# Loads issued three attention tiles ahead of use, with buffers dealt anew and the order rebuilt

## The chip, the cores and the metric

The kernel runs on one core of one Trainium2 chip. A time is the device time of one execution in microseconds (us). Medians are over the executions named; the fast executions of one kernel lie within about 1.5% of each other here. A run counts as slow when it is over 1.5% above the fastest run of the same kernel; slow runs are left out of every comparison. Traces are of one execution each. The span of a trace is some 1.7 us shorter than the time of the same execution (287.6 against 289.32 us in before).

## The reference, cut to what matters

Block-sparse attention over 4 batches of 8 heads, 768 tokens, head size 64; its output, as 3,072 rows of 512, goes through a two-layer network with a swish-like gate.

```python
scores = scale * np.matmul(q, k.transpose(0, 1, 3, 2))
scores = np.where(mask, scores, -1e9)          # mask of 32x32 blocks, from an input
attn = softmax(scores)                          # along the keys
x = np.matmul(attn, v)                          # -> [3072, 512]
h = x @ w_in                                    # [3072, 2048]
out = (h * sigmoid(beta * h)) @ w_out           # [3072, 512]
```

## The kernel before

Two heads make a pair; there are 16 pairs, numbered 0 to 15, four to a batch. A pair's K, Q and V are loaded as float32 (384 KB each), cast to float16 on VectorE (DVE) or GpSimd (POOL), and K and Q are transposed, by TensorE (PE) for the first four pairs and by the DMA engines for the rest. A tile is 256 or 512 queries of one pair; it takes 3 or 6 score steps (scores on PE, exponential on ScalarE (ACT), mask on DVE), then the product with V, a normalization on DVE and a transpose of the result. Batches are numbered from zero. As soon as enough tokens are done, the network's two layers run on PE: "up" with `w_in`, "down" with `w_out`.

The program is a list of nodes. A greedy builder, `order_of`, sorts them with a model of durations, buffers and DMA rates before anything runs. It takes the node with the smallest modelled start plus a bias for its kind. The program then gives each engine its nodes strictly in that order. So changing a bias, a buffer count or a modelled size rebuilds the order on all engines.

```python
BIAS = {"mask": -288, "spread": 115, "beta": 289, "weights": 285, "load": 963, "cast": 110, ...}
W_GATE = (2, "k")
SLOTS = {"st_k": 3, "st_q": 4, "st_v": 3, "s16_k": 2, "s16_q": 3, "set": 6, "va": 7,
         "et": 12, "xst": 4, "recip": 4, "t_sb": 4, "g": 2, "osb": 3, "sc": 2, "mm": 4}
# st_*: float32 stagings of loads; s16_*: float16 casts; set: transposed K and Q of a pair;
# va: V in float16; xst: attention output; osb: final output

def order_of(nodes, free, slots):
    ...
                key = (n_start + n.dur[e] - min(n.dur.values()) + bias, n.place)
                if best is None or key < best[0]:
                    best = (key, n, e, n_start)
    ...

def add_weights(gate):                 # W_GATE: the load after which the weights start
    st, load = gate
    def shut():                        # a tiny op that waits for that load
        nc.gpsimd.tensor_copy(out=w_in_sb[0:1, 0, 0:1], in_=at(st)[0:1, 0, 0:1])
    gate = add("weights", "POOL", 600, 50, shut, deps=[load], use=[st])
    ...                                # then four loads of weights from POOL's queue, 1 MB each
                                       # as written in float16

def add_load(nm, x, st, lo, hi, gate): # from SP's queue
    ...
    deps = [(last_load[0], -1e9)] if last_load else []
    ...
    last_load[:] = [add("load", "SP", ..., load, deps=deps,
                         moved=65536 * (hi - lo) + ..., **kw)]

for x in range(NPAIR):                 # batch zero: K, part of Q, V of pairs 0..3
    add_prep(x)
add_weights(loads[W_GATE])
for x in range(NPAIR):                 # the rest of Q of pairs 0..3
    add_rest(x)
for x in range(NPAIR, len(pairs)):     # all other pairs: as early as buffers allow
    add_prep(x, (0, 1, 1) if x == NPAIR else (None, None, None))
...
for b, q0, n in tiles:
    for j in range(NPAIR):
        ...                            # score steps and tail of one tile
```

The softmax here doesn't subtract the row's maximum and nothing guards it: scores larger than these inputs give would overflow.

## Time and profile before

| | before |
|---|---|
| time, median of 3 | 291.43 us (290.86 to 291.66) |
| span of the trace | 287.6 us |
| PE busy | 265.2 us, idle 22.4 us |
| DVE, ACT busy | 209.4 us, 212.9 us |

The page of the kernel before: first busy time, share of the span and count of instructions; then 40 equal slices of 7.2 us, each digit the busy share in tenths; PEclk is the granted clock of PE in tenths, DMA the busy share of the DMA engines, GB/s what they moved.

```profile
span 287.6 us, 6162 instructions
...
PE 265.2 (92%) x2455; PEld 138.1 (48%) x2455; DVE 209.4 (73%) x429; ACT 212.9 (74%) x277; POOL 27.6 (10%) x46
...
PE   4767899979895999899999999999999999999994
...
PEclk9998999999999999999999999999999999999999
DMA  7999987999999997771227201021002111011112
GB/s 205 291 232 214 212 182 197 279 237 223 230 269 234 252 282 153 173 164 28 76 73 131 55 2 55 20 93 55 1 2 73 39 43 43 0 21 73 39 44 105
```

PE is full from about 120 us on. Up to about 108 us, while the DMA engines move mostly 200 to 290 GB/s, it is not. The busy time in chosen stretches (start:end and length, then busy us of PE, PEld, DVE, ACT and POOL with counts, granted clock, DMA share, GB/s) says how much is missing where:

```profile
20.00:41.00 21.00, 17.91 (x193) 12.00 (x194) 17.47 (x43) 18.81 (x31) 0.87 (x3) 0.92 1.15 212
41.00:60.00 19.00, 17.79 (x209) 9.33 (x205) 17.74 (x39) 16.81 (x21) 2.13 (x4) 1.00 1.00 220
60.00:120.00 60.00, 52.86 (x506) 26.09 (x505) 46.52 (x90) 44.96 (x56) 10.80 (x12) 1.00 1.13 229
120.00:279.00 159.00, 159.00 (x1416) 81.23 (x1414) 113.69 (x216) 119.75 (x159) 4.16 (x5) 1.00 0.21 54
```

From 60 to 120 us PE lacks 7.1 us. The timeline (start, duration, engine, line, operation, in brackets the engine's idle time before it and what ended it) shows the largest piece:

```profile
88.72 0.56 DVE L394 CAST va<-st_v 128x768 f16<-128x768 f32 x1 [4.72 <-DMA st_v<-in_v_dram]
...
89.20 0.42 DVE L522 TENSOR_TENSOR xst<-mm,recip 128x256 f16<-128x256 f32 x1
...
89.67 2.89 PE L586 MATMUL mm<-w_out_sb,g 128*128 128x512 f16 x12 [3.27 <-DVE xst L522]
...
92.92 1.94 ACT L468 ACTIVATE et<-sc 128x1024 f16<-128x1024 f32 x2 [4.76 <-PE sc L460]
```

DVE stood 4.72 us before the cast of a V, because its load had not landed (it did at 88.70 us). The normalization `xst` that stood behind the cast in DVE's order came only at 89.20; it releases a PSUM buffer, and the down matmuls of PE waited 3.27 us for that. This V belongs to pair 10, whose first scores come at about 137 us: nobody needed the cast yet. In this trace the mask and normalization work behind the cast did not pass it: DVE stood idle for those 4.72 us, and `xst` began 0.48 us after the cast.

### The profile page before, as it was taken

Reading aid. Unit: us, or ns where it says so; the run is one execution under the profiler, and the core shown is the slowest. Engines: PE = TensorE matmul, PEld = TensorE weight load, DVE = VectorE, ACT = ScalarE, POOL = GpSimd, SP = SyncE. Lnnn points to the kernel's source line nnn. Section 1 sums busy time; section 2 is a strip of 40 time slices with the busy share of each in tenths; the row PEclk is TensorE's granted clock in tenths of the full one; section 3 lists DMA queues with packets and bytes.
Section 4 is the critical chain, followed back from the end, with each engine's and each line's share of the span. In section 5 each row is a group of like instructions: output and inputs, shape, how many; then the busy total and the mean of one; then the engine's idle time right before and its main releaser. Section 6 shows DMA issues by size and latency. Waiting matters only on the chain.

```text
span 287.6 us, 6162 instructions
## 1 busy us (share of the span) xinstructions
PE 265.2 (92%) x2455; PEld 138.1 (48%) x2455; DVE 209.4 (73%) x429; ACT 212.9 (74%) x277; POOL 27.6 (10%) x46
## 2 busy tenths in 40 slices
PE   4767899979895999899999999999999999999994
PEld 1545575443362365346455336363345454466741
DVE  5878888998966586999688886587877686852600
ACT  1688997999863777897888997679976888824621
POOL 4520101111431001113001000000000000000000
PEclk9998999999999999999999999999999999999999
DMA  7999987999999997771227201021002111011112
GB/s 205 291 232 214 212 182 197 279 237 223 230 269 234 252 282 153 173 164 28 76 73 131 55 2 55 20 93 55 1 2 73 39 43 43 0 21 73 39 44 105
DMA packets 72850, 36.66 MB, mean 127 GB/s; under 512 B 29796, under 2 KB 68724, under 8 KB 72820
## 3 DMA queue, kind: packets, MB, share of 16 engines
q1 hardware_dynamic: 69568, 32.06, 49.0%
q0 software_dynamic: 3136, 4.19, 8.2%
q8 instruction: 19, 0.31, 0.5%
q14 instruction: 11, 0.09, 0.1%
q10 hardware_dynamic: 116, 0.01, 0.0%
HBM read 27.27 MB, written 6.29 MB: 117 GB/s over the span
## 4 chain that ended last, share of the span: by engine, by line
PE 71%; DMA 13%; DVE 7%; SPq 3%; ACT 2%; issue 1%; POOL 0%; DVEq 0%; POOLq 0%; ACTq 0%
PE mm L586 27%; PE mm L562 24%; PE mm L512 10%; PE sc L460 10%; DMA st_q<-in_q_dram 9%; DVE et L477 3%; ACT et L468 2%; DMA kX<-s_k 2%; SPq L410 1%; DMA sb_i<-in_sampled_blocks_dram 1%; DMA st_k<-in_k_dram 1%; SPq L374 1%; DVE g L571 1%; DVE s_k L394 1%; SPq L371 1%
## 5 line engine op out<-in xcount | busy, mean ns | idle before, releaser
L468 ACT ACTIVATE et<-sc 128x1024 f16<-128x1024 f32 x144 | 141.4, 1027 | 35.2 <-PE sc L460 33.8
L477 DVE TENSOR_TENSOR et<-et,mask 128x1024 f16<-128x1024 f16 x144 | 99.9, 701 | 22.9 <-ACT et L468 22.6
L586 PE MATMUL mm<-w_out_sb,g 128*128 128x512 f16 x384 | 93.1, 380 | 3.3 <-DVE xst L522 3.3
L562 PE MATMUL mm<-xT_sb,w_in_sb 128*128 128x512 f16 (+1 forms) x448 | 90.7, 349 | 2.8 <-DVE g L571 2.3
L567 ACT ACTIVATE t_sb<-mm,beta_h_sb 128x512 f16<-128x512 f32 (+1 forms) x112 | 67.4, 635 | 15.7 <-PE mm L562 15.2
L571 DVE SCALAR_TENSOR_TENSOR g<-t_sb,mm 128x512 f16<-128x512 f16 (+1 forms) x112 | 65.2, 606 | 18.1 <-ACT t_sb L567 17.6
L562 PEld LDWEIGHTS <-w_in_sb 128*128 128x128 f16 x448 | 42.2, 98 | 47.6 <-issue 11.2
L586 PEld LDWEIGHTS <-g 128*128 128x128 f16 x384 | 34.0, 98 | 47.6 <-issue 14.9
L460 PE MATMUL sc<-qX,kX 64*128 64x256 f16 (+1 forms) x384 | 47.3, 338 | 5.0 <-ACT et L468 3.0
L512 PEld LDWEIGHTS <-et 128*128 128x128 f16 x1152 | 41.1, 99 | 8.4 <-issue 1.2
L512 PE MATMUL mm<-va,et 128*128 128x65 f16 x1152 | 43.3, 195 | 1.0 <-DVE osb L598 0.7
L460 PEld LDWEIGHTS <-kX 64*128 64x128 f16 x384 | 15.2, 95 | 28.8 <-issue 23.1
L596 ACT ACTIVATE osb<-mm 128x512 f32<-128x512 f32 x14 | 8.4, 599 | 16.5 <-PE mm L586 16.3
L522 DVE TENSOR_TENSOR xst<-mm,recip 128x256 f16<-128x256 f32 x48 | 20.0, 419 | 0.6
L519 DVE RECIPROCAL recip<-mm 128x4 f32<-128x4 f32 x48 | 8.4, 177 | 4.0 <-PE mm L512 3.5
L394 POOL CAST s_q<-st_q 128x768 f16<-128x768 f32 (+2 forms) x9 | 7.5, 835 | 38.5 <-PE mm L562 16.5
L394 POOL CAST s_k<-st_k 128x768 f16<-128x768 f32 x7 | 5.8, 830 | 45.3 <-DMA st_k<-in_k_dram 26.3
L394 DVE CAST va<-st_v 128x768 f16<-128x768 f32 x10 | 5.8, 576 | 5.8 <-DMA st_v<-in_v_dram 5.8
L394 DVE CAST s_q<-st_q 128x768 f16<-128x768 f32 (+2 forms) x11 | 5.7, 514 | 4.1 <-DMA st_q<-in_q_dram 3.8
L394 POOL CAST va<-st_v 128x768 f16<-128x768 f32 x6 | 5.5, 920 | 30.7 <-PE mm L512 23.1
L598 DVE TENSOR_SCALAR osb<-mm 128x512 f32<-128x512 f32 x10 | 6.8, 685 | 0.0
L540 DVE COPY xT_sb<-mm 128x256 f16<-128x256 f16 (+1 forms) x10 | 3.6, 357 | 4.3 <-PE mm L535 4.3
(52 smaller groups left out, 44.8 us busy)
## 6 DMA issues: line engine op xcount, KB each, us to landing
st_k<-in_k_dram SPq DMA_DIRECT2D x16, 384.0 KB, 5.1
st_v<-in_v_dram SPq DMA_DIRECT2D x16, 384.0 KB, 5.4
out_dram<-osb SPq DMA_DIRECT2D x24, 256.0 KB, 2.0
st_q<-in_q_dram SPq DMA_DIRECT2D x12, 384.0 KB, 6.1
w_in_sb<-in_moe_w_in_dram POOLq DMA_DIRECT2D x2, 1024.0 KB, 13.2
w_out_sb<-in_moe_w_out_dram POOLq DMA_DIRECT2D x2, 1024.0 KB, 22.2
st_q<-in_q_dram SPq DMA_DIRECT2D x12, 128.0 KB, 5.6
xT_sb<-xst SPq DMA_TRANSPOSE x22, 2.6
```

The lines of the kernel that those rows point to most:

```text
L394: e(out=at(dst)[:, :, :, 0:D] if nm == "v" else by_chunk(dst, lo, hi), in_=src)
L460: nc.tensor.matmul(at(sc)[:, hh, i * n:(i + 1) * n], lhsT=kX[hh * D:(hh + 1) * D, (kc0 + i) * P:(kc0 + i + 1) * P], rhs=qX[hh * D:(hh + 1) ...
L468: nc.scalar.activation(out=at(et).rearrange("p h q -> p (h q)"), in_=at(sc).rearrange("p h q -> p (h q)"), func=AF.Exp, bias=0.0, scale=SCALE)
L477: nc.vector.tensor_tensor(out=e, in0=e, in1=m, op=ALU.mult)
L512: nc.tensor.matmul(a[:, i, hh, :], lhsT=at(ets[kc // kn])[:, hh, at0:at0 + P], rhs=at(va)[:, hh, kc, 0:D + 1], start=(kc == 0), stop=(kc = ...
L519: nc.vector.reciprocal(out=at(rb), in_=av_ap()[:, :, :, D:D + 1])
L522: nc.vector.tensor_tensor(out=at(xs)[:, half * 2:half * 2 + 2], in0=av_ap()[:, :, :, 0:D], in1=at(rb).to_broadcast([P, 2, 2, D]), op=ALU.mult)
L562: nc.tensor.matmul(at(hb)[:, 0:n], lhsT=w_in_sb[:, c, f * P:(f + 1) * P], rhs=xT_sb[:, c, t0:t0 + n], start=(c == 0), stop=(c == NPAIR - 1))
L567: nc.scalar.activation(out=at(tb)[:, 0:n], in_=at(hb)[:, 0:n], func=AF.Tanh, bias=0.0, scale=beta_h_sb[:, f:f + 1])
L571: nc.vector.scalar_tensor_tensor(out=at(gb)[:, f, 0:n], in0=at(tb)[:, 0:n], scalar=1.0, in1=at(hb)[:, 0:n], op0=ALU.add, op1=ALU.mult)
L586: nc.tensor.matmul(at(ob), lhsT=at(gb)[:, f, ts * P:(ts + 1) * P], rhs=w_out_sb[:, f, :], start=(f == 0), stop=(f == N_FFC - 1))
L596: nc.scalar.activation(out=at(sb), in_=at(ob), func=AF.Copy, bias=0.0, scale=0.5)
```

## The change

The intent: the loads of a pair enter the list when the tile three before the pair's first tile starts its scores. Buffers are dealt anew, the model's load is made heavier, and the biases are new. Not an instruction of arithmetic is added or removed.

```diff
-BIAS = {"mask": -288, "spread": 115, "beta": 289, "weights": 285, "load": 963, "cast": 110, ...}
+BIAS = {"mask": -376, "spread": 460, "beta": 362, "weights": 409, "load": 1106, "cast": 18, ...}
+AHEAD = 3
-    SLOTS = {"st_k": 3, "st_q": 4, "st_v": 3, "s16_k": 2, "s16_q": 3, "set": 6, "va": 7,
-             "et": 12, "xst": 4, "recip": 4, "t_sb": 4, "g": 2, "osb": 3, "sc": 2, "mm": 4}
+    SLOTS = {"st_k": 4, "st_q": 4, "st_v": 4, "s16_k": 3, "s16_q": 2, "set": 4, "va": 8,
+             "et": 12, "xst": 5, "recip": 3, "t_sb": 4, "g": 2, "osb": 4, "sc": 2, "mm": 4}
-        deps = [(last_load[0], -1e9)] if last_load else []
+        deps = [(d, -1e9) for d in last_load + begin]
-                             moved=65536 * (hi - lo) + (500000 if x == 0 and nm == "v" else 0),
+                             moved=73000 * (hi - lo) + (500000 if x == 0 and nm == "v" else 0),
-    for x in range(NPAIR, len(pairs)):
-        add_prep(x, (0, 1, 1) if x == NPAIR else (None, None, None))
+            begin[:] = [sc_of[i * NPAIR + j]]      # first score step of this tile
+            for y in range(NPAIR, len(pairs)):
+                if first_unit[y] == i * NPAIR + j + AHEAD:
+                    add_prep(y, (0, 1, 1) if y == NPAIR else (None, None, None))
 ...  # numbering of tiles, and sc_of, cut
```

The dependence on the score step has a lag of minus 1e9: it puts the load behind that step in the builder's list. It is no wait on the chip.

More of the change, by code (lines that the diff above doesn't have):

```diff
@@ L38, in __init__ @@
         self.start = self.done = self.on = None
-BIAS = {"mask": -288, "spread": 115, "beta": 289, "weights": 285, "load": 963, "cast": 110,
-        "dma": -659, "turn": 69, "turn cp": 125, "sc": -30, "next sc": -293, "lone sc": 106,
-        "ex": 240, "mk": 63, "av": 40, "norm": 9, "x turn": 37, "x cp": -282, "hp": 31, "op": 57,
-        "op on": 82, "th": 187, "gm": -28, "osb": 157}
+BIAS = {"mask": -376, "spread": 460, "beta": 362, "weights": 409, "load": 1106, "cast": 18,
+        "dma": -489, "turn": 22, "turn cp": 117, "sc": -59, "next sc": -271, "lone sc": 111,
+        "ex": 260, "mk": 137, "av": 41, "norm": 9, "x turn": -35, "x cp": -218, "hp": 39,
+        "op": 43, "op on": 62, "th": 247, "gm": -7, "osb": 57}
 W_GATE = (2, "k")
 SLACK = 1500.0
+AHEAD = 3
 HOP = 60.0
@@ L338 @@
     w_in_of, w_out_of, loads = {}, {}, {}
-    last_load = []
+    last_load, begin = [], []
     def add_weights(gate):
@@ L481, in tile_steps, with add_step @@
         return steps, ets
-    def add_step(step):
+    sc_of = {}
+    def add_step(step, unit):
         x, q0, sc, et, mm, ex, mk, masks = step
@@ L488, in add_step @@
                 take=[sc], use=[r["kq"]], rows=64)
+        sc_of.setdefault(unit, g)
         e = add("ex", "ACT", 927, 100, ex, deps=[g], take=[et], use=[sc])
@@ L623 @@
     upto, gi = 0, 0
-    for b, q0, n in tiles:
+    units = [(b * NPAIR + j, q0, n) for b, q0, n in tiles for j in range(NPAIR)]
+    first_unit = {}
+    for u, (x, _, _) in enumerate(units):
+        first_unit.setdefault(x, u)
+    for i, (b, q0, n) in enumerate(tiles):
         for j in range(NPAIR):
@@ L629 @@
             for st in steps:
-                masked.append(add_step(st))
+                masked.append(add_step(st, i * NPAIR + j))
             add_tail(x, q0, n, ets, masked)
+            begin[:] = [sc_of[i * NPAIR + j]]
+            for y in range(NPAIR, len(pairs)):
+                if first_unit[y] == i * NPAIR + j + AHEAD:
+                    add_prep(y, (0, 1, 1) if y == NPAIR else (None, None, None))
         upto = b * S + q0 + n
```

## The prediction

> **What bounds it now.** TensorE. The page shows it busy 265.2 of 287.6 us (92%). Busy time in 10-us windows: from 120 us to the last window it has no gap; before 120 us it is busy 101.2 us, so 18.8 of the 22.4 idle us lie there. The slices show the DMA engines near saturation to 120 us (mostly 200 to 290 GB/s) and little used later. Batch two is fetched from 67 us on, far ahead of use: the V load landing at 88.7 us is of a pair first scored at about 137 us.
>
> The first 31 us hold about 10 us of TensorE idle time: exponentials (1.03 us each), first loads and weights set the pace. About 8.5 us more lie between 57 and 118 us. In the timeline, the largest piece: VectorE stands 4.72 us before the cast of that V, whose load was late; normalizations behind it in VectorE's order hold PSUM buffers, and TensorE stands 3.27 us, ScalarE 4.76. Others: 1.21 us at 57.9 (score matmuls paced by exponentials), 0.78 at 62.8, 1.24 at 70.6, 0.67 at 99.5, 1.18 at 117.1.
>
> **What the change does.** Arithmetic stays: 2,455 matmuls, 144 exponentials, the same casts and bytes. I compared the built orders. Score blocks[...] go from 73 to 74; the last 100 us of TensorE order nearly stay. What moves:
> - Loads of batches two and three are issued about one pair at a time, between transposes and stores. Batch one's still come at once, behind the weights, at about 41 to 65 us.
> - Four sets instead of six: a pair's transpose waits for the last scores of the pair four before, by order done some 15 us of TensorE work before need.
> - Four stagings per tensor: fewer waits of loads for buffers.
> - The order's model charges a load 1.44 us instead of 1.29; back-to-back loads land 1.3 to 1.5 us apart in the trace. [...] an early load for a distant pair delays what queues behind it.
> - Scores run further ahead at the start (22 steps instead of 17 before the first up-projection).
>
> **On the critical path.** Only the 8.5 us between 57 and 118 us, and perhaps 1 us at the start. I expect the 3.27-us stall to go, as distant prefetch goes, and about half of the rest, against about 1.5 us of new waits: batch two's transposes now queue behind output transposes and stores, and pair 8 has by order only about 3 us of slack (estimate from traced matmul durations). Net 3.7 us.
>
> **Predicted: 287.7 us, 80% range 283.5 to 291.8.** Faster by over 2%: 0.25; within 2%: 0.72; slower by over 2%: 0.03.
>
> **Would show it right.** TensorE idle 18 to 20 us, its busy time unchanged within 1 us; DMA slices lower between 65 and 90 us and busy later, to about 200 us; VectorE's wait for V loads under 2 us; no 3-us gap near 88 us. First 41 us about as before; no gap after 130 us.
>
> **Would make it wrong.** Just-in-time loads late at the start of batch two (gaps of several us near 95 to 120 us): then 291 or slower. Or the rebuilt order also removing most of the starting idle time: then below 284.

What the trace of before does show is this. Eight output matmuls and a block take 2.37 us (from 141.81 to 144.18 us), and 128x512 matmuls in a row start 0.216 us apart. The transfers that SP issues land in the order of their issue, wherever a landing is on record: three loads at 81.66, 83.02 and 84.36 us, for example. A transpose that was issued at 85.18 us behind three loads landed 6.77 us later; one that was issued at 158.91 us with no load in flight landed after 2.77 us.

## The result, and the profile after

| | before | after |
|---|---|---|
| time, median | 291.55 us (4 runs, one slow) | 286.57 us (286.55 to 286.75, 4 runs) |
| ratio, fast runs | 1 | 0.9838, 95% interval 0.9819 to 0.9858 |
| span of the trace | 287.6 us | 284.8 us |
| time of the traced execution | 289.32 us | 286.56 us |
| PE busy, idle | 265.2, 22.4 us | 265.2, 19.6 us |

Ratios are the mean time of one kernel's fast runs over that of the other's fast runs of the same rounds, so they are not quite the ratio of the medians quoted. In later rounds (chips 2, 9 and 10), before took 288.87 to 293.35 us when fast. The one traced execution of before, at 289.32 us, was faster than every timed one beside it (290.86 us and more). So the two traces are 2.8 us apart and the medians 4.9 us; the traces below explain the 2.8, and what took the other 2 us in the timed executions is not on record. The result was correct, as was that of every experiment below.

The same parts of the page of the kernel after, in the same order:

```profile
span 284.8 us, 6153 instructions
...
PE 265.2 (93%) x2455; PEld 138.7 (49%) x2455; DVE 209.4 (73%) x434; ACT 212.2 (74%) x278; POOL 24.6 (9%) x41
...
PE   4782889998999999999999999999999999999994
...
PEclk9996699999999999999999999999999999999999
DMA  7999983699602057899476984651002111011112
GB/s 203 291 229 213 213 177 102 156 244 261 135 1 39 37 166 154 208 283 203 111 209 135 232 196 93 182 135 56 0 2 74 39 49 37 0 21 74 39 45 103
```

And its stretches:

```profile
20.00:41.00 21.00, 13.18 (x134) 7.93 (x132) 14.18 (x34) 14.47 (x18) 1.49 (x4) 0.76 1.15 214
41.00:60.00 19.00, 18.52 (x237) 11.68 (x235) 18.31 (x46) 15.86 (x25) 0.92 (x3) 1.00 0.59 146
60.00:120.00 60.00, 59.23 (x571) 29.43 (x571) 50.55 (x97) 52.73 (x67) 4.74 (x5) 1.00 0.56 129
120.00:279.00 159.00, 158.88 (x1385) 80.92 (x1383) 111.75 (x214) 117.63 (x158) 8.48 (x11) 1.00 0.42 103
```

Two opposite things happened. From 60 to 120 us PE is now busy 59.23 instead of 52.86 us. From 20 to 41 us it is busy 13.18 instead of 17.91 us, and there the granted clock is 0.76 instead of 0.92. The DMA engines move 1 to 39 GB/s between about 78 and 100 us, where before they moved over 220. The timeline of after shows the loss (line numbers are up to 4 higher than before's for the same code: the cast is L395, the mask L478, the exponential L469, the score L461, the TensorE transpose L419):

```profile
27.38 0.43 DVE L395 CAST s_q<-st_q 128x512 f16<-128x512 f32 x1 [4.93 <-DMA st_q<-in_q_dram]
27.72 1.29 DVE L478 TENSOR_TENSOR et<-et,mask 128x1024 f16<-128x1024 f16 x2
...
27.87 0.61 PE L419 MATMUL mm<-identity,s_q 128*128 128x128 f16 x4 [4.97 <-DVE s_q L395]
...
29.06 2.85 ACT L469 ACTIVATE et<-sc 128x1024 f16<-128x1024 f32 x3 [4.84 <-PE sc L461]
```

This is the same pattern as before's at 88.72 us, at another place: DVE stands 4.93 us before a cast, this time of the rest of Q of pair 1, and PE and ACT stand with it. Added up over the whole trace by instruction, the gaps of PE are 10.27 us before the start of the 33rd up matmul and 8.53 us after it in the kernel before, and 14.82 and 1.21 us in the kernel after. So the later part gained 7.3 us and the start lost 4.5 us; the difference is the 2.8 us between the two spans.

### The profile page after: what moved, and what is told of

Its sections match the earlier page's. It is cut to its first block, busy times and chain, and to the rows that moved or that the text cites. A ratio compares the mean times of both kernels' runs of the same rounds, so it can differ in the third digit from the quotient of the medians.

```text
span 284.8 us, 6153 instructions
## 1 busy us (share of the span) xinstructions
PE 265.2 (93%) x2455; PEld 138.7 (49%) x2455; DVE 209.4 (73%) x434; ACT 212.2 (74%) x278; POOL 24.6 (9%) x41
## 4 chain that ended last, share of the span: by engine, by line
PE 84%; DMA 5%; SPq 4%; DVE 3%; ACT 1%; issue 0%; DVEq 0%
PE mm L590 30%; PE mm L566 28%; PE mm L516 13%; PE sc L461 12%; DMA st_q<-in_q_dram 5%; SPq L372 2%; SPq L375 2%; DVE et L478 2%; ACT et L469 1%; DVE g L575 1%; PE mm L539 1%; PE mm L419 0%; DVE xst L526 0%; ACT osb L600 0%; DVE s_q L395 0%
## 5 line engine op out<-in xcount | busy, mean ns | idle before, releaser
L469 ACT ACTIVATE et<-sc 128x1024 f16<-128x1024 f32 x144 | 141.1, 1026 | 34.4 <-PE sc L461 32.0
L478 DVE TENSOR_TENSOR et<-et,mask 128x1024 f16<-128x1024 f16 x144 | 99.0, 694 | 23.0 <-ACT et L469 22.2
L590 PEld LDWEIGHTS <-g 128*128 128x128 f16 x384 | 34.0, 98 | 43.5 <-issue 10.8
L461 PE MATMUL sc<-qX,kX 64*128 64x256 f16 (+1 forms) x384 | 48.4, 342 | 5.3 <-ACT et L469 4.0
L461 PEld LDWEIGHTS <-kX 64*128 64x128 f16 x384 | 15.6, 96 | 30.2 <-issue 25.5
L600 ACT ACTIVATE osb<-mm 128x512 f32<-128x512 f32 x19 | 11.5, 604 | 17.3 <-PE mm L590 11.7
L395 POOL CAST s_q<-st_q 128x768 f16<-128x768 f32 (+1 forms) x8 | 7.3, 910 | 64.2 <-DMA st_q<-in_q_dram 59.5
L395 DVE CAST s_q<-st_q 128x768 f16<-128x768 f32 (+2 forms) x12 | 5.3, 445 | 8.5 <-DMA st_q<-in_q_dram 6.3
L419 PE MATMUL mm<-identity,s_q 128*128 128x128 f16 x24 | 3.5, 272 | 5.5 <-DVE s_q L395 5.5
L395 POOL CAST s_k<-st_k 128x768 f16<-128x768 f32 x4 | 3.3, 826 | 48.4 <-DMA st_k<-in_k_dram 48.4
L395 DVE CAST s_k<-st_k 128x768 f16<-128x768 f32 x12 | 7.2, 597 | 0.0
L395 POOL CAST va<-st_v 128x768 f16<-128x768 f32 x5 | 4.4, 883 | 22.5 <-DMA st_v<-in_v_dram 22.5
L395 DVE CAST va<-st_v 128x768 f16<-128x768 f32 x11 | 6.2, 568 | 0.0
## 6 DMA issues: line engine op xcount, KB each, us to landing
w_out_sb<-in_moe_w_out_dram POOLq DMA_DIRECT2D x2, 1024.0 KB, 23.7
```

Of the source, the lines that this page charges most:

```text
L395: e(out=at(dst)[:, :, :, 0:D] if nm == "v" else by_chunk(dst, lo, hi), in_=src)
L461: nc.tensor.matmul(at(sc)[:, hh, i * n:(i + 1) * n], lhsT=kX[hh * D:(hh + 1) * D, (kc0 + i) * P:(kc0 + i + 1) * P], rhs=qX[hh * D:(hh + 1) ...
L469: nc.scalar.activation(out=at(et).rearrange("p h q -> p (h q)"), in_=at(sc).rearrange("p h q -> p (h q)"), func=AF.Exp, bias=0.0, scale=SCALE)
L478: nc.vector.tensor_tensor(out=e, in0=e, in1=m, op=ALU.mult)
L590: nc.tensor.matmul(at(ob), lhsT=at(gb)[:, f, ts * P:(ts + 1) * P], rhs=w_out_sb[:, f, :], start=(f == 0), stop=(f == N_FFC - 1))
L600: nc.scalar.activation(out=at(sb), in_=at(ob), func=AF.Copy, bias=0.0, scale=0.5)
```

## The experiments

Two questions: what emptied the later stretch of gaps, and what put gaps into the start. For the first, theory A is that the later loads themselves bring the gain; its rival, theory B, is that the new biases and buffers bring it. Further theories are named where they are tested. To keep them apart, a table at the end of this section gives, for each traced run, the time from the start of the 33rd up matmul to the start of the last down matmul, called the stage. Each value comes from one trace; three traces with the same order after the start (`a_late`, `late_again`, `late_early`) agree within 0.1 us, but a half-clock stretch inside a stage, where a run has one, adds to it (in the stretch of after, from 23.7 to 33.9 us, 128x65 matmuls in a row start 0.055 us apart, outside it 0.032; medians). The marker is not perfect: kernels with the new biases have done 25 score steps by then, those with the old 20. The five steps are 1.5 to 2 us of PE (an estimate: a block of one step takes 0.39 us, of two 0.60 in the traces), so stages are compared within one set of biases where it matters.

### The part "three ahead" alone, and everything but it

`b_ahead` is the kernel before with the load placement of after and nothing else; `a_free` is after with its load placement taken back.

```diff
# b_ahead: after, with
-BIAS = {... new ...}                    +BIAS = {... before's ...}
-SLOTS = {... new ...}                   +SLOTS = {... before's ...}
-moved=73000 * (hi - lo)                 +moved=65536 * (hi - lo)
# a_free: after, with
-            begin[:] = [sc_of[i * NPAIR + j]]
-                if first_unit[y] == i * NPAIR + j + AHEAD:
+                if i == j == 0:
```

> The kernel before with one part of the change alone: loads issued with the tile three ahead; its own buffers, biases and bytes per load. Built order: the same as before's through the first 37 entries of the load queue (all of batch one but the last pair), so nothing may differ before about 60 us. Theory A (the gain comes from taking distant prefetch out of the stretch from 57 to 118 us, where its late casts block VectorE): the 3.27-us TensorE gap near 89 us goes, the gaps of that stretch fall from about 8 to under 4 us, 286 to 288.5 us. Theory B (the gain comes from the rebuilt order, that is biases and buffers; when the loads go out matters little): within 1 us of before, 290.5 to 292.5.

> The kernel after with that one part undone: all loads as early as buffers allow, with its four sets, its stagings, its biases and its 73,000 bytes per chunk. The first 40 us of order are the same. Theory A: VectorE waits for loads of batch two again between 60 and 115 us, TensorE gaps of 3 to 6 us in that stretch, 289.5 to 292.5 us. Theory B: within 1 us of after, 285.6 to 287.6.

Measured: `b_ahead` 289.43 us (289.22 to 290.85), ratio to before 0.9989 (0.9942 to 1.0036), beside runs of before with a median of 290.61. That is neither the 286 to 288.5 us of theory A nor quite theory B's range (290.5 to 292.5 us). The 3.27-us gap near 89 us did go, and after the start DVE waits for a load only once, for 0.4 us; it was 6.0 us ahead of before at the 161st up matmul. But it gave this back between 150 and 157 us, where scores come one step at a time, each waiting for an exponential. The timeline of `b_ahead`:

```profile
152.74 0.39 PE L461 MATMUL sc<-qX,kX 64*128 64x512 f16 x2 [0.92 <-ACT et L469]
153.66 0.39 PE L461 MATMUL sc<-qX,kX 64*128 64x512 f16 x2 [0.53 <-ACT et L469]
154.58 0.39 PE L461 MATMUL sc<-qX,kX 64*128 64x512 f16 x2 [0.53 <-ACT et L469]
```

PE does 0.39 us of work in 0.92 us here; a half-clock stretch of 3.4 us follows. The builder, with loads that come later and old biases, had put matmuls of the down layer in front (160 of them are done before the 95th score step, the one at 152.74 us, and 148 before the same step in the kernel before), and then nothing was left to fill the waits between score steps.

`a_free`: 291.19 us (288.92 to 291.43), ratio to before 1.0018. Theory A's range. Its start is like that of after (0.5 us apart), and it loses 4.8 us in the stage: 3.5 us more of gaps, and a half-clock stretch at 112 us. The timeline of `a_free`:

```profile
109.91 0.56 DVE L395 CAST s_q<-st_q 128x768 f16<-128x768 f32 x1 [3.48 <-DMA qX<-s_q]
...
110.38 1.28 DVE L478 TENSOR_TENSOR et<-et,mask 128x1024 f16<-128x1024 f16 x2
...
111.12 1.11 PE L516 MATMUL mm<-va,et 128*128 128x65 f16 x28 [2.48 <-DVE et L478]
```

Again a cast at the head of DVE's order. But what it waits for is not its load: it waits until a DMA transpose has emptied the float16 buffer that it writes. That transpose was itself late: it was issued at 103.85 us, behind V of pair 13 and K of pair 14 (issued at 101.29 and 103.30 us, landed at 107.80 and 109.06), and landed at 109.81, 6.0 us after its issue; a transpose of after with no load in flight took 2.8 us (113.94 to 116.75). A gap of 1.13 us at 99.9 us has the same origin: a cast waited 1.44 us for a transpose that landed 5.7 us after its issue, behind another load.

### Only the late casts moved

`b_cast` is before, with three casts of far-off pairs later in DVE's order; nothing else moves.

```diff
+    for tag, left in [((12, "q", 0), 8), ((11, "q", 0), 8), ((10, "v", 0), 9)]:
+        ...    # take that cast out of seq, put it `left` instructions of its engine later
```

> The kernel before, with three casts of batch-two and batch-three loads (V of pair 10, Q of pairs 11 and 12) put eight or nine instructions later in VectorE's order; every other engine's order and all loads are the same. If the 4.72-us stand of VectorE before the cast of that V is what held TensorE (theory A's mechanism): the 3.27-us gap near 89 us shrinks to under 1 us and the time falls by 1.5 to 3.3 us, to 288 to 290. If the stretch is held by the DMA engines or by the order as such, the same time is lost a little later: within 0.7 us of before.

Measured: 291.5 us (290.84 to 291.83), ratio 1.0047. The gap of 3.27 us is gone, so the cast's stand was its cause. But the time is lost 20 us later, as the second theory said; it even came out about 1 us slower than before, where that theory allowed 0.7 us either way. Its timeline:

```profile
90.07 0.56 DVE L394 CAST va<-st_v 128x768 f16<-128x768 f32 x1 [0.29 <-DMA st_v<-in_v_dram]
...
110.32 0.38 PE L564 MATMUL mm<-xT_sb,w_in_sb 128*128 128x512 f16 x1 [2.05 <-DMA xT_sb<-xst]
...
115.09 0.56 DVE L394 CAST s_q<-st_q 128x768 f16<-128x768 f32 x1 [6.60 <-DMA qX<-s_q]
...
116.30 1.25 PE L564 MATMUL mm<-xT_sb,w_in_sb 128*128 128x512 f16 x4 [2.08 <-DVE g L573]
```

DVE stands 6.60 us at 115 us, and up matmuls also wait 2.05 and 0.77 us for DMA transposes of attention output; the first of these had been issued at 105.55 us behind six loads, the last of which landed at 108.52. The stage is 248.0 us, as in before. One late cast is the place at which the time was lost, not the amount.

### Which of the other two parts: biases or buffers

```diff
# a_biasB: after, with before's biases;  a_slotsB: after, with before's buffers
-BIAS = {... new ...}                    +BIAS = {... before's ...}
-SLOTS = {... new ...}                   +SLOTS = {... before's ...}
```

> The kernel after with before's biases: loads three tiles ahead, four sets, the new stagings and 73,000 bytes per chunk stay. Measured from the 33rd up-projection matmul to the last output matmul (that leaves out the start, which varies by 2 us from run to run), before took 248.0 us, after 238.5, loads three ahead alone 246.3, buffers and biases alone 243.3. If the new buffers are what lets the later loads pay, this run takes 239 to 242 us in that stretch; if the rebuilt biases are, 244 to 247 us, with scores in a row paced by exponentials as in the run with the loads alone (five gaps of 0.5 to 0.9 us at 152 to 157 us).

> The kernel after with before's buffers (six sets, three, four and three stagings): loads three tiles ahead, new biases and 73,000 bytes stay. If the biases are what lets the later loads pay: 239 to 242 us in the stretch from the 33rd up-projection to the last output matmul; if the buffers are: 244 to 247 us, with loads or transposes waiting for a free buffer.

Measured: `a_biasB` 287.95 us, ratio 0.9931 (0.9882 to 0.9979), stage 243.2 us; `a_slotsB` 287.6 us, ratio 0.9912 (0.9862 to 0.9961), stage 238.4 us. The second is plain, as far as one trace goes: with three-ahead loads and the new biases, before's buffers do as well as the new ones (238.4 against 238.5), and gaps after the start are 1.12 us. The first lies between its two expected ranges, just under the one for the biases (244 to 247); part of its distance to 238.5 is the five score steps of the marker, and part a half-clock stretch of 3.4 us at 63.8 us. It has 2.6 us of gaps, paced by exponentials at 62 to 68 us.

### Does an early load cost anything by itself?

All variants so far rebuild the order when the loads move. `late_early` does not. It starts from the kernel `a_late` (below: after, with the weights started later), and moves only the twelve loads of batch two in the load queue, about 27 us forward or more. Order on all compute engines, casts and transposes stay.

```diff
+    early = [m for m in seq if tag(m)[:1] == ("load",) and 8 <= tag(m)[1] < 12]
+    seq = [m for m in seq if m not in early]
+    to = ...                     # behind the last transpose and cast of batch one
+    seq[to:to] = early
```

> After with the late weights, and the twelve loads of batch two moved in the load queue to directly behind batch one's last transpose (issue at about 70 instead of 97 to 121 us); the order on every compute engine is the same, so are all casts and transposes. Theory Q (early loads cost by themselves, by what queues behind them): output transposes of batch one and the stores come late, the time rises by 1 to 4 us. Theory O (early loads cost nothing by themselves where the DMA engines have room, as here from 70 to 90 us; what cost 4.8 us in the run with the loads set free was the order built around them, with casts and transposes too early on VectorE and in the queue): within 0.7 us of the run beside it.

> After with the late weights once more, beside the run above on the same chip: 280.5 to 282.5 us, ratio to before 0.965 to 0.975.

Measured, on one chip, five timed rounds: `late_early` 282.29 us (ratio to before 0.9694, 0.9635 to 0.9754), `late_again` 281.69 us (0.9663, 0.9611 to 0.9716); the 0.6 us between them is within both intervals. The traces decide it. The stage is 238.3 us in `late_early` and 238.4 us in `late_again` and `a_late`; the gaps after the start are 1.1 us in all three. The page of `late_early`, whose slices are 7.0 us:

```profile
PE   4786899989999999999999999999999999999994
...
GB/s 190 291 261 214 207 178 167 250 262 212 237 292 223 60 69 103 133 21 84 65 237 191 191 177 156 166 80 39 0 21 57 40 50 38 0 51 45 51 65 75
```

From 49 to 91 us the DMA engines move over 200 GB/s, as in before at that time, and PE has no gap of note there. So theory O (it is the order that costs, not an early load) holds for this batch: issuing its loads early cost nothing by itself (a stage of 238.3 against 238.4 us). The output transposes that did queue behind these loads came a little late (one took 3.7 us from issue to landing, against 2.4 in `late_again`), and nobody waited for them. The run does not clear early loads where urgent work queues behind them: in `a_free` the transposes behind loads were late, and the casts waited for those. What costs in `a_free` is then, by its trace, the order that the builder makes around early loads: casts of far-off pairs stand on DVE long before their time, and wait for transposes that stand in the queue behind loads. No run separates these two halves.

### What put gaps into the start

The trace of after gives the landings of the eight loads of the rest of Q (two for each of pairs 0 to 3, 128 KB each; one of the eight has no landing on record). They share the DMA engines with the weights (four loads of 1 MB as written), which POOL's queue issues.

| landing of the rest of Q, us | pair 0 | pair 1, second | pair 2 | pair 3 |
|---|---|---|---|---|
| before | 16.62, 16.98 | 23.93 | 27.18, 29.69 | 31.55, 33.52 |
| after | 16.90, 20.60 | 27.29 | 29.60, 31.55 | 33.41, 35.36 |
| a_late | 17.25, 17.70 | 18.58 | 19.00, 19.43 | 23.41, 26.56 |

Before the weights flow, a load lands every 0.43 us or so; while they flow, every 1.9 to 4.0 us. The packet records in the trace files, which no view prints, show what lies between: in the trace of after, 256 packets of weights and 255 of SP's queue start from 17 to 20 us, and 597 and 594 from 20.60 to 27.29 us. But these packets are unequal: from 17 to 20 us one of the weights has 2,048 bytes and takes 172 ns, one of a Q load 512 bytes and 40 ns. A load of 128 KB is 256 such packets; with as many of the weights that is 256 times 212 ns on the 16 engines that the page counts, about 3.4 us (an estimate from these figures; 3.35 us on average in the trace of after, between 20.60 and 27.29 us). In before, two loads got past ahead of the weights, in after only one (weights issued 0.26 us earlier, the loads 0.3 us later), and so all others came about one place later. Pair 1's rest landed at 27.29 us, and its cast stood first in DVE's order.

`a_late` changes the wait of one instruction: the weights start after K of pair 3 instead of pair 2, about 3 us later. The built order is the same on every engine. `b_late` does the same to before.

```diff
-            nc.gpsimd.tensor_copy(out=w_in_sb[0:1, 0, 0:1], in_=at(st)[0:1, 0, 0:1])
+            nc.gpsimd.tensor_copy(out=w_in_sb[0:1, 0, 0:1], in_=at(loads[3, "k"][0])[0:1, 0, 0:1])
```

> The kernel after with one wait changed: the weights' first load waits for K of the fourth pair instead of K of the third (about 3 us later); the order on every engine is the same. Theory S1 (the kernel after loses 5 us at 23 to 28 us because the second Q load of pair 1 shares the DMA engines with the weights and lands at 27.3 us, and the cast of it stands first in VectorE's order): the Q loads land by about 21 us, the 4.97-us gap falls under 1.5 us, the half-clock stretch falls from 10.2 to at most 6.8 us, the time falls by 4 to 7 us, to 280 to 282.5; the weights land at about 41 us as now. Theory S2 (the start is paced by exponentials and by the order): less than 1 us of change, or slower, as the weights come later.

> The kernel before with one wait changed, as in the run that made after 5.65 us faster: the weights wait for K of pair 3 instead of K of pair 2. In before's order other work stands ahead of the late casts (its largest gap in the start is 0.7 us in the traced run, 2.0 and 2.6 us in two runs that share its start). If the 5.65 us were mostly a fault of the order of after that the late loads exposed, before gains 1 to 3 us: 288 to 290. If late weights are worth as much whatever the order, it gains 4 us or more: under 287.

Measured: `a_late` 281.22 us (280.83 to 282.54), ratio to before 0.9704 (0.9656 to 0.9751); its repeat is `late_again` above. In the trace it is 5.7 us ahead of after at the first up matmul (32.0 against 37.6) and as far ahead at the end: nothing else of note changed. The timeline of `a_late`, to be read against that of after:

```profile
22.46 0.42 DVE L395 CAST s_q<-st_q 128x512 f16<-128x512 f32 x1
...
22.89 0.39 PE L461 MATMUL sc<-qX,kX 64*128 64x512 f16 x2 [0.52 <-DVE s_q L395]
```

The cast that had stood 4.93 us starts at once. Two things make up the 5.7 us: PE's gaps before the stage fall from 14.8 to 10.8 us, and its busy time falls from 265.2 to 263.6 us with the half-clock stretch, which was 10.2 us in after and is absent here. The weights land 1.7 us later (42.45 us), still before the first down matmul (44.5). The last two Q loads came at 23.41 and 26.56 us, not by 21 as expected; nothing waited long for them. Theory S1, that the start is lost to the weights' share of the DMA engines, holds. How large the gain is in timed runs is less sure, as after and `a_late` were not run side by side: by the medians it is 5.3 us, by the ratios to before (0.9838 and 0.9704) about 3.9.

How far the half clock is a consequence of that gap stays open. The clock records in the trace files, which no view prints, give a granted clock of 0.5 in stretches of 3.4 us (before, from 26.5 us), 6.8 us (`late_again`, from 24.4 us) and 10.2 us (after, from 23.7 us). A long gap just before them does not account for their beginnings: the stretch of after begins only 0.8 us into the gap, before has no gap over 0.7 us from 9 us up to its stretch, and `late_again` has none over 1 us near its own. Later on, single gaps of 2.48 us (`a_free`, at 111.1 us) and of 2.05 us (`b_late`, at 97.0 us) were followed within 1.2 us by a stretch of 3.4 us at half clock, while a gap of 3.27 us (before, at 89.7 us) was not: its granted clock is 1.00 from 60 to 120 us. `a_late` and `late_again` are one kernel; without a stretch and with one of 6.8 us they reach the 33rd up matmul at 36.8 and 38.7 us. So these stretches are at least part of why the first 40 us vary between runs.

`b_late` came out at 288.08 us (287.19 to 290.16), ratio 0.994 (0.9859 to 1.0021), in the range expected if the 5.7 us were mostly a fault of after's own order; the interval reaches 1, so a gain for before is not shown.

### Other leads, and a rebuilt order

```diff
# late_ahead2, late_ahead4: a_late, with
-AHEAD = 3                               +AHEAD = 2    (4)
# gate3k: after, with the builder told of the later start
-W_GATE = (2, "k")                       +W_GATE = (3, "k")
```

> After with the late weights (281.2 us in its own run), and the loads two tiles ahead instead of three; the order is rebuilt, the same through the first 40 us or so of score blocks. If three is near the least lead that hides load, cast and transpose (some 15 to 20 us from issue of the loads to the first score in the traced kernel after): transposes of batch two land late, TensorE gaps of 1 to 4 us between 95 and 160 us, 282.5 to 286 us. If the exact lead does not matter as long as distant prefetch is gone: within 1 us of 281.2.

> The same with four tiles ahead. A whole batch is four pairs, so this is still near use, and the four sets hold it back anyway. Theory A as refined (it is the unlimited prefetch that costs, in the load queue ahead of the output transposes): within 1.5 us of 281.2, stretch from the 33rd up-projection to the last output matmul 237.5 to 240 us (238.4 with three). If each tile more of lead costs: 283 or more.

> The late weights told to the order builder, so that the whole order is rebuilt for them, instead of the wait alone changed under the same order. The start can gain at most 1 to 2 us more (what remains of its 10.8 us of gaps is 5.5 us before the first scores and pacing by exponentials), but a rebuilt order changes everywhere: 279 to 284 us.

Measured: `late_ahead2` 286.36 us (286.3 to 288.91), stage 243.2; `late_ahead4` 284.86 us (284.1 to 285.89), stage 240.2; `gate3k` 282.07 us (281.11 to 282.57), stage 238.4. Two expectations failed. With two ahead I had expected transposes to land late. PE waits for no load and no transpose; what its gaps have beyond those of `a_late` is mostly five pauses of 0.5 to 0.9 us between scores at 148 to 157 us, each ended by an exponential, as in `b_ahead`. With four ahead I had expected no difference, and it is 3.6 us slower than `a_late` was on another chip, 1.8 us of it in the stage; the rest is its start, with two half-clock stretches. `gate3k` came out in its expected range: a rebuilt order gained nothing over the changed wait alone. Since the biases came with a lead of three, these runs do not show that three is best as such.

### The stage of all variants

| run | loads | buffers | biases | 33rd up matmul, us | stage, us | PE gaps after it, us |
|---|---|---|---|---|---|---|
| before | free | old | old | 35.6 | 248.0 | 8.5 |
| b_cast | free | old | old | 37.9 | 248.0 | 7.1 |
| b_late | free | old | old | 34.9 | 247.6 | 6.9 |
| b_ahead | 3 ahead | old | old | 37.4 | 246.3 | 5.3 |
| a_biasB | 3 ahead | new | old | 38.7 | 243.2 | 2.6 |
| a_free | free | new | new | 42.0 | 243.3 | 4.7 |
| a_slotsB | 3 ahead | old | new | 42.8 | 238.4 | 1.1 |
| after | 3 ahead | new | new | 42.4 | 238.5 | 1.2 |
| a_late | 3 ahead | new | new | 36.8 | 238.4 | 1.1 |
| late_early | batch two early | new | new | 36.9 | 238.3 | 1.1 |

Three ahead is worth 1.7 us with the old biases and buffers, and 4.8 us with the new ones (of which a half-clock stretch in `a_free` is a part; `a_free` also has two float16 buffers for Q where before has three, and it was not run with before's buffers). Each part is worth more with the other; the new buffers, given the other two, are worth nothing measurable.

## Why the prediction was right or wrong

- **The time**: 287.7 us was predicted, 286.57 measured; faster by 1.6%. Inside the range, and within 2%. The net gain of 3.7 us that was predicted from the trace lies between the 2.8 us of the traces and the 4.9 us of the medians.
- **What bounds it, and PE's work**: right. Busy time is 265.2 us in both traces. Idle time 19.6 us, where 18 to 20 was said.
- **"I expect the 3.27-us stall to go ... and about half of the rest, against about 1.5 us of new waits"**: the direction was right, the size too small on both counts. Gaps after the start fell from 8.5 to 1.2 us, and there are no new waits in batch two: the 3 us of slack that I had estimated for pair 8 sufficed.
- **"an early load for a distant pair delays what queues behind it"**: true by the trace of before (6.77 us from issue to landing behind three loads, 2.77 with none in flight), but no cost by itself. With the order held, loads of batch two issued some 30 us earlier changed nothing (238.3 against 238.4 us), as nobody waited for what queued behind them. By its trace, it cost in `a_free`, where a transpose queued behind such loads and a cast that stood early in DVE's order waited for that transpose (6.0 us from issue to landing, 3.48 us of waiting). So the order decides, and the deferral works by what the builder makes of it.
- **"Perhaps 1 us at the start", "first 41 us about as before"**: wrong, and the largest error. The start lost 4.5 us in gaps; one cast stood 4.93 us for a load slowed by the weights. The prediction compared the orders there and not when the second Q loads would land beside the weights. That scores run further ahead there, as I had read from the order, is true (25 steps instead of 20 at the same up matmul); it could not help while DVE stood.
- **The checks**: DMA slices lower (though from 72 us on, not from 65) and busy later, no wait for V on DVE, no gap near 88 us, none over 0.15 us after 130 us: as predicted.

So the total was right by luck in part, with two errors that cancel: a gain of 7.3 us in gaps, where the net 3.7 and the 1.5 of new waits make about 5, and a loss of 4.5 us that was not foreseen. What remains open: how much of the biases' share belongs to the 73,000 bytes, which were not tried alone, how the cost of early loads divides between early casts on DVE and late transposes in the queue, and what starts a half-clock stretch in the first 40 us. The best version is `a_late`: 3.0 and 3.4% faster than before in two sets of runs.

## What to carry to other kernels

Here an early cast of data that nobody needed yet was a wait placed in front of work that was needed (DVE stood 4.72 us before it, and PE 3.27 us); look for it as idle time of the engine that ends with a DMA, while others wait for that engine. When a static order is rebuilt, compare the traces stretch by stretch, because a gain in one and a loss in another can hide each other in the total, and the loss may be a single wait. Let small loads that are needed soon pass before a large transfer begins on another queue: here 128-KB loads landed every 0.43 us before the weights flowed and every 1.9 to 4.0 us beside them. Letting the loads pass made the large one land 1.7 us later, still before its use, and the time was 281.2 and 281.7 us in two sets of runs, against 286.57 for after in a third.
